# A newly searched order and engine choice for an attention and mixing kernel of 2292 operations

## The chip, the cores and the metric

The kernel runs on one core of a Trainium2 chip. It uses TensorE (PE) for matrix products, VectorE (DVE), ScalarE (ACT) and GpSimd (POOL) for elementwise work, and SyncE (SP) to issue all DMA transfers. The metric is device microseconds of one execution; the three runs of the kernel before gave 484.78, 487.29 and 488.31 us.

## The reference

Block attention over 4 batches, 8 heads, 768 positions and 64 columns a head: each query sees its neighbours within 15 positions and one summary (maximum of the keys, mean of the values) of each block of 32. The result `x` of 4 x 768 x 512 goes through a mixing layer:

```python
theta = x @ w_theta
zr, zi = x * cos(theta), x * sin(theta)
y = w_tok_r @ zr + w_tok_i @ zi          # over the 768 positions
u = x + y
return u + maximum(u @ w_ch, 0.0)
```

The weights `w_theta`, `w_tok_r`, `w_tok_i` and `w_ch` arrive as 64-bit floats and are turned into 32-bit ones by integer operations on the device.

## The kernel before

Every product that needs full precision is made of three matmuls on operands that are split in two: a high part, which is a cast of the 32-bit number to the matmul's reduced format, and a low part, the number minus its high part. So each operand costs a cast (`hi_op`, lines 307 on ScalarE and 309 on VectorE or GpSimd) and a subtraction (`lo_op`, line 316, on VectorE or GpSimd).

The work goes through these stages, overlapping each other:

- Loading and preparing. `to_f32` (lines 399 to 410) turns the weights into 32-bit numbers: an absolute value (399 on ScalarE, 401 on VectorE), a clamp (403), a shift (405), and two joinings (407 and 410).
- Attention, 24 tiles of 128 queries: scores (line 521), the running maximum (557), the exponential (561), transposes (570) and their copy out (574), the product with the values (544), normalising (582 to 591). Keys and values are copied into place by lines 493 and 498.
- Theta and the turn, per tile: transposes of `x` (600), their copies (307, 309, 606), the product with `w_theta` (631, 636), the reduction of the angle (647 to 655), sine and cosine (659, 660), the product with `x` (666).
- Mixing. The first two batches take the plain product (line 694). The last two use a scheme with seven products instead of eight (`mix_fast`, line 809): its operands are made in tiles `zu` by sums and differences (`add_op`, line 722) and split into tiles `hl`; its weights come back from a scratch tensor into the tiles `wt`; the results are added to `x` by line 818.
- Output. The product with `w_ch` uses seven products too (`out_batch`, line 914): operands are made from `u` by line 722 into tiles `cb` and split into tiles `wt`. For the first two batches `u` is loaded back into tiles `cu`; for the last two it is still in `x`. The channel weights are combined in the same way (tiles `zu`, `cb`, `wth`). The sums of the products are formed by lines 921 and 926, and line 933 makes the final result, which SP writes out.

An operand of the output is ready only when its cast and its subtraction are done; the products of line 914 and then the evictions of lines 921 to 933 wait for them. The banks in PSUM in which the products of line 809 gather are freed by line 818.

What sets the order is the table `ORDER`: each word is the number of an operation, in the order in which the program issues them; every engine takes its own in that order and does not pass a waiting one. A letter behind a number chooses the engine (`a` ScalarE, `d` VectorE, `g` GpSimd); without one the engine with the smallest assumed cost is taken:

```python
for word in ORDER.split():
    o = self.ops[int(word.rstrip("padg"))]
    o.eng = dict(p="PE", a="ACT", d="DVE", g="POOL").get(word[-1]) or min(o.cost)
    order.append(o)
```

When the instructions are laid down, a GpSimd operation that works on SBUF alone and follows directly, among such operations, on one of VectorE gets a wait for it (`port` in the last loop of `attn_moe`):

```python
if o.eng in o.port:
    mine = [i for i in traced[n:] if i.engine == units[o.eng]]
    if o.eng == "POOL" and port:
        tc.add_manual_dep(mine[0], port.name, ...)
    port = mine[-1] if o.eng == "DVE" else None
```

Of the kernel before, what the change touches and what calls it, by code (L numbers as in the profile page):

```python
# [54 lines left out]
23 0 1 24 14 8 27 17g 18 9 31 2 25 29 10 3 4 39 28 79 26 44g 5 33 30 32 19 6g 35 20 46g 45 49 7g 15 50 239 48g 47g 80d 190g 51  # L55
60 61 62 52 21 192g 11 81g 54 55 34 65 53 66 194g 63 82 86 36 64 67 185 193g 59 12 40 238g 83 191 87 42 56 37 93 84 38g 235 58
100 188 88 195 57 13 89 90 186 43 70 41 68 69 71d 204 206 295g 207 211 94 72 205 208 107 91 73d 293g 196 210 241g 76 240g 199
108 198 200 197 290 74 294g 22 77 95g 209 187g 202 92g 203 189g 242 75d 78d 237 96 201 214 212 223 243 101 215 97 246 245 213
236 102g 296g 98 216 85g 244 350g 103 99g 111 224 104 251 348g 225 247 118 254 119g 105 217 226 252 253 255 227 248 220d 218
106g 250 292 221 256 228 219d 249 123 222d 124g 349g 257 258 259 120 705g 229 261 121 262 297 125 260 230 270 126 298 231 263  # L60
300 271 272 304 122 273 109 306 308 345 110 309 301 307 141 291 264 265 267 268 113 351g 302 142g 274 299 266d 305 310 313 303
130 275 112 312 311 131g 707g 127 276 269d 314 143 316 144 315 419 317 352 135 277 325 318 132 326 136g 709g 232 286g 327 422g
133 347 328 329 114 425g 319 145 115 278 134 152 361 279 153g 362 128 353 330 355 146 116 147g 366 233 137 364 356 282 320 234
322 154 280 359 357 155 423g 283 346 138 284 323 285 363 339 367 139 281 368 156 331 354 321d 157 337 158g 324 338 424g 148
163 360 365 358 529 159 369 164g 149 332 371 380 150 160 370 372 426 165 381 333 420 421 334 373 427 166 400 382 161 167 374d
383 168 117 404 435 401 377 378 384 385 386 375 169g 170 174 340 335 171 175g 394 474 392 387 376 379 405 140 179 454 703g 393
# [12 lines left out]
700 818 676 702 728 649d 651 675 652d 840 795 819 580g 844g 686 684 685 687 796 753 850 725g 688 689d 1020 756 577 820 757 821
690 765 851g 766 975 691 761 581 729 730 800 822 1015 767 759 694 852g 845g 731 732 1021 976d 797 945 977 695 768 582 946 978  # L80
760 771 692 846d 979 770 801 693d 847g 823 802 980 758 769 726 848 853 749 762 764 763 804 772 981 824 803 854 806 849 573 810
855 750 798g 982 856g 696 943 941 775 983 776d 773 859 860g 861g 826d 947 774 984 956 777 960 805 995 825 948 862g 808 778d
828 996 858 829 799g 998 781 959 997 957 809 999 830 952 751 951 1000 857 1018 1001 949 958 950 831 782 953 779 963 961 863g
962 868 780d 985 955 954 811 783d 944d 1022 1023 986 964 966 1019 942g 1002 864g 967d 965 865g 1026 991 968 1003 827 866 1025
969 1004 1050 1031 1033 869g 870 993 1053 1051 1016 992 970 871g 1052 972d 867 877 807 1037 872g 1076 1024 1054 1027 1035 994
1074 1034 873 987 1129 1028 988 973 1077 1055 1030 878g 1038 1032 971 1036 989g 875 1005d 974d 1013 879 1056 1029 1041 1039
1057 1042d 1011 1058 1106g 1078 1017g 1059 874g 1079 1040 1170 1043 876 990g 886 1173 1120g 880g 1006 1208 1209 1211 1087 1047
1080 1060 1081 1044d 881 1088 1127 1210 1012 1082 1091 1014 1084 882g 1128 1083 1085 884 1089 1212 1048 1007 887 1092 1090
1045 1008 1086 1066 1046 888g 1075 1213 883 1049d 889g 1009g 1068 1214 1094 1126 1107g 1095 885 1093 895 1061 1097 1215 1096d
1067 1098d 1216 1010 890g 1062 891g 1130 1099 1217 1218 1219 896 893 1279 892g 1069 1131 1282 1139 1100 1064 1134 1070 1133  # L90
1143 1072 1280d 1140 1281 1135 897 1142 1132 1221 1144 1065g 1141 1145 1283 1101 1073 894 1284 1285 904 1136 1063 1103 898
1137 1102d 1247 899g 1138 1146 1071 1286 900g 1104 1158 1105d 901 1287 1149 1147 905g 906g 1174 1150 1148d 1288 1151 907 1305
1108 1152 1183 1220 1306 1110 1175 1121g 1185 1308 1171 1172 903 1153 1307 1179 1154d 908g 1309 1178 1176 1109 1177 909 902
910g 1184 1181 1250 1310 1155 1187 913 912 1111 1182 1289d 1156 1311 1180 1157d 1164g 1186 914g 1188 1189 1191 1118 1251 1190
1193 915g 1192 1116 1112 1312 1114 1313 911 916g 922 1122 1194d 1260 917g 1195 918g 1314 1199 1252 1262 1354 1123 1124 1125
1256 1355d 1159g 923 920 1357 919 921 1290 1162 924g 925g 1356 1358 1113 926 1315 1253 1257 931 1222 1165 1292 1249 927g 1160
1291 1196 1255 928g 929 1161 1359 1163 1197 1261 1265 1360 1223g 1168 1266 1228 1254 932g 1200 1202d 1316 933 1361 1166 1167
1264 1169 1263 1362 1258 1259 1198d 1599g 1267 1201d 1320 1268 1363 934g 1318 1593 1368 1270 1364 935g 1229 1204 1369d 930
1322 1370 1600g 1371d 1230 1248 936 1206 1372 1203g 938 1365 1271d 1231 1205 1317 1236 1373 937 1207 1237 1234 1117 1587g 1269
1374 1672 1594g 1366 1235 1232 1272 1240 1588g 1226 1227 1273 1276 1375 1376 1277 1274 1377 1275 1233 1295 1224 1278d 1319  # L100
1367 1225 1417 1418 1324g 1420 1325 1378d 1238 1293 1241 1294 1419 1421 1242 1385 1387 1296 1422 1379 1297 1589g 1301 1675
1595g 1302 1644 1243 1645 1299 1303 1423 1646 1424 1239 1244 1326 1425 1603g 1647 1658 1590 1388 1426 1327 1596g 1660 1427
# [1012 lines left out]
```

## Time and profile before

| | |
|---|---|
| runs | 484.78, 487.29, 488.31 us |
| the profiled execution | 484.78 us; its span, from the first to the last instruction, 483.0 us |
| TensorE (PE) busy | 440.1 us (91%) |
| VectorE (DVE) busy | 391.3 us (81%) |
| ScalarE (ACT) busy | 254.3 us (53%) |
| GpSimd (POOL) busy | 271.3 us (56%) |

Busy times are those of the engines' own instructions; waits and the issuing of DMAs do not count. A row of the windows gives them for one stretch. A row of the groups gives the line, the engine, the operation, what it writes and reads, the count, the busy time, the mean duration of one in ns, and the idle time of the engine ahead of them with what ended it. PEclk is the granted TensorE clock as a share of its full level.

### The profile page before, as it was taken

The page shows a single profiled execution, that of the slowest core. Times are in us where ns is not written, and L with a number is a line of the kernel's source. Part 1 is how long each engine was busy: PE and PEld are TensorE (multiplying, and loading weights), DVE is VectorE, ACT ScalarE, POOL GpSimd, SP SyncE. Part 2 cuts the span into 40 slices and gives each one's busy share as a digit, 9 for nine tenths or more (in the row PEclk, how much of TensorE's full clock was granted, in tenths as well). Part 3 has the DMA queues.
Part 4 walks back from the last instruction along what each step waited for, and adds up shares of the span by engine and source line. Part 5 has one row for each costly group of instructions (what it writes and reads, how often), then busy time and mean ns, then how long its engine had stood idle before and what let it go on. Part 6 is the DMA issues. An engine that isn't in the chain of part 4 may idle for free. (4 is left out here: it accounts for less than half of the span.)

```text
span 483.0 us, 9649 instructions
## 1 busy us (share of the span) xinstructions
PE 440.1 (91%) x3490; PEld 363.4 (75%) x3490; DVE 391.3 (81%) x940; ACT 254.3 (53%) x534; POOL 271.3 (56%) x262
## 2 busy tenths in 40 slices
PE   5969999999989999999999999999994966995997
PEld 1446555667868888888889899989894866985896
DVE  3899999798599565886768867667999989888896
ACT  1769886665578678756835534784420311331030
POOL 3595522636295646565532973231557788599550
PEclk9999999999999999999999999999997988998899
DMA  8999767897847798666688869441954744010037
GB/s 299 314 299 339 261 219 227 245 339 230 288 138 214 223 249 262 192 195 196 199 267 262 264 200 269 148 153 58 359 161 166 247 145 131 16 67 0 34 127 280
DMA packets 76318, 100.03 MB, mean 207 GB/s; under 512 B 23024, under 2 KB 58864, under 8 KB 76272
## 3 DMA queue, kind: packets, MB, share of 16 engines
q1 hardware_dynamic: 76272, 99.43, 65.4%
q8 instruction: 27, 0.44, 0.4%
q14 instruction: 19, 0.16, 0.1%
HBM read 75.82 MB, written 23.59 MB: 206 GB/s over the span
## 5 line engine op out<-in xcount | busy, mean ns | idle before, releaser
L809 PE MATMUL m<-wt,hl 128*128 128x384 f32 x504 | 99.3, 350 | 8.2 <-DVE x L818 8.0
L809 PEld LDWEIGHTS m<-wt,hl 128*128 128x128 f32 x504 | 91.5, 196 | 11.7 <-DVE x L818 8.1
L694 PE MATMUL m<-wt,hl 128*128 128x512 f32 (+1 forms) x432 | 83.7, 340 | 0.0
L694 PEld LDWEIGHTS m<-wt,hl 128*128 128x128 f32 x432 | 68.2, 188 | 10.7
L561 ACT ACTIVATE e<-e,st 128x118 f32<-128x118 f32 x192 | 62.8, 386 | 18.5 <-DVE st L557 18.0
L557 DVE CUSTOM_DVE_ANT_0 e<-s,cs 128x118 f32<-128x118 f32 x192 | 45.7, 272 | 11.4 <-PE s L521 10.3
L316 POOL TENSOR_TENSOR hl<-zu,hl 128x512 fp32r<-128x512 f32 x32 | 43.5, 1365 | 17.8 <-DVE hl L309 8.5
L636 PE MATMUL t<-wth,xh 128*128 128x512 f32 x144 | 47.1, 408 | 0.1
L722 POOL TENSOR_TENSOR zu<-zu 128x512 f32<-128x512 f32 x22 | 30.1, 1373 | 23.2 <-DVE zu L666 12.0
L666 DVE TENSOR_TENSOR zu<-xn,zu 128x512 f32<-128x512 f32 x48 | 37.2, 788 | 3.3 <-ACT zu L660 3.1
L722 POOL TENSOR_TENSOR f<-f 128x192 f32<-128x192 f32 x35 | 22.9, 656 | 29.8 <-DVE zu L666 13.9
L309 POOL CAST hl<-zu 128x512 fp32r<-128x512 f32 x24 | 16.0, 670 | 36.1 <-PE m L809 17.2
L694 PE MATMUL m<-wt,zu 128*128 128x512 f32 (+1 forms) x96 | 33.1, 491 | 0.5 <-DVE zu L666 0.4
L647 ACT ACTIVATE zu<-t,bmagic 128x512 f32<-128x512 f32 x24 | 16.5, 687 | 30.6 <-PE t L636 25.2
L307 ACT CAST hl<-zu 128x512 fp32r<-128x512 f32 x23 | 14.2, 617 | 32.0 <-PE m L809 17.7
L570 PE MATMUL pa<-cs,e 128*118 128x128 f32 x192 | 26.5, 275 | 4.6 <-DVE xn L591 2.8
L544 PEld LDWEIGHTS pa<-v,e 118*64 118x64 f32 x768 | 24.6, 137 | 6.9 <-issue 3.3
L544 PE MATMUL pa<-v,e 118*64 118x65 f32 x768 | 28.1, 224 | 1.5 <-ACT e L574 0.8
L694 PEld LDWEIGHTS m<-wt,zu 128*128 128x128 f32 x96 | 17.6, 190 | 15.7 <-issue 12.6
L316 DVE TENSOR_TENSOR hl<-zu,hl 128x512 fp32r<-128x512 f32 x28 | 27.7, 996 | 2.0 <-ACT hl L307 1.5
L570 PEld LDWEIGHTS pa<-cs,e 128*118 128x118 f32 x192 | 21.4, 136 | 10.1 <-issue 2.6
L636 PE MATMUL t<-wth,xl 128*128 128x512 f32 x72 | 28.5, 395 | 0.0
(189 smaller groups left out, 975.2 us busy)
## 6 DMA issues: line engine op xcount, KB each, us to landing
wt<-s_scratch SPq DMA_DIRECT2D x48, 384.0 KB, 4.8
v<-vg SPq DMA_DIRECT2D x48, 195.0 KB, 4.3
s_scratch<-f SPq DMA_DIRECT2D x24, 384.0 KB, 3.1
k<-kg SPq DMA_DIRECT2D x18, 376.0 KB, 5.3
q<-qg SPq DMA_DIRECT2D x24, 256.0 KB, 4.3
wt<-wtr SPq DMA_DIRECT2D x6, 768.0 KB, 10.7
wt<-wti SPq DMA_DIRECT2D x6, 768.0 KB, 11.8
f<-kT SPq DMA_DIRECT2D x12, 384.0 KB, 3.5
```

The costliest lines, as they stand in the source:

```text
L309: V[e].tensor_copy(dst(), src())
L316: lambda e: V[e].tensor_tensor(dst(), src(), hi().bitcast(F32), op=ALU.subtract), reads, writes, due, port=BOTH)
L544: mm(2 * 0.433 + scores[0] + (0.2 if scores[0] else 0.0), [lambda n=n, g=g, a=a: nc.tensor.matmul(xa[a].get()[ROW[g], n], turned[a].get()[ ...
L557: op({"DVE": 0.205}, lambda eng, n=n: nc.vector.tensor_tensor_reduce(e()[:, n], sc[n % 2].get()[:, 2 * a + n // 2], mask(m), -SCALE, 3.0e3 ...
L561: op({"ACT": 0.288}, lambda eng, n=n: nc.scalar.activation(e()[:, n], e()[:, n], AF.Exp, bias=st.get()[:, n:n + 1], scale=-1.0), [(st, n)] ...
L570: mm(NH * 0.109, [lambda n=n: nc.tensor.transpose(tp.get()[:NK, n], e()[:, n], ident()) for n in range(NH)], [e_ref, (cs, "ident")], [tp], ...
L636: calls = [lambda t=t, xx=xx, k=k, c=c: nc.tensor.matmul(th.get(), xx.get()[:, c], w_th[c].get()[:, k], start=(c == 0 and t == 0), stop=(c ...
L647: op({"ACT": 0.59}, lambda e: nc.scalar.activation(r(), th.get(), AF.Identity, bias=bmagic.get(), scale=1.0), [th, bmagic], R, due)
L666: op({"DVE": c_dve(DM, "two")}, lambda e, z=z, hc=hc: nc.vector.tensor_tensor(z(), xn[b, i].get().rearrange("p h d -> p (h d)")[:, None, h ...
L694: nc.tensor.matmul(acc[th](), zz, w[:, TT[th]], start=(s == 0 and r == 0 and t == 0 and (th == 0 or c == 0)), stop=(s == NT - 1 and r == 1 ...
L722: lambda e: V[e].tensor_tensor(dst(), x(), y(), op=ALU.add if sign > 0 else ALU.subtract), reads, writes, due, port=BOTH)
L809: calls = [lambda ref=ref, tt=tt, z=z, s=s, j=j, t=t, x=x, k=k, bank=bank, first=first: nc.tensor.matmul(bank[j].get()[:, :HT], z.get()[:, ...
```

## The change

Only the table `ORDER` is changed: all its 86 lines are new. The operations are the same 2292; their order differs, and 312 of them stand on another engine. In the built program GpSimd has 193 instructions where it had 267, ScalarE 621 where it had 536, VectorE 958 where it had 942; TensorE has 2641 and SP 289 in both.

```diff
 ORDER = """
-23 0 1 24 14 8 27 17g 18 9 31 2 25 29 10 3 4 39 28 79 26 44g 5 33 30 32 19 6g 35 20 46g 45 49 7g 15 50 239 48g 47g 80d 190g 51
...
-2263 2283 2168 2285 2203 2279 2267 2289 2268 2284 2286 2280 2287 2290 2288 2269 2291 2270
+17 31 23 25 0g 24 1g 27 29 18 11g 39 8g 19 26 44 20 28 46 45 9 2 33 86 10 48 3 30 4 5 49 21 190g 35 79 6g 47 185 32 7g 50 51
...
+2269 2270
 """
```

The engines' own orders show what that means. The first place is on GpSimd, where the operands of the last fast mix (`hl`, `zu`) end and the operands of the output stage (`cb`, `cu`, `wt`, `wth`) begin. Before:

```order
L722 TENSOR_TENSOR cb<-cu 128x768
L722 TENSOR_TENSOR zu<-zu 128x2x256
L316 TENSOR_TENSOR hl<-zu,hl 128x512
L309 CAST hl<-zu 128x512
L316 TENSOR_TENSOR hl<-zu,hl 128x512
L722 TENSOR_TENSOR zu<-zu 128x2x256
L309 CAST hl<-zu 128x512
L309 CAST wth_4516<-zu 128x512
L722 TENSOR_TENSOR cb<-zu 128x2x256 x2
L316 TENSOR_TENSOR hl<-zu,hl 128x512
L722 TENSOR_TENSOR cb<-cb,zu 128x2x256
L309 CAST wt<-cb 128x768
```

After, the same place, to near the end of GpSimd's queue:

```order
L722 TENSOR_TENSOR zu<-zu 128x2x256
L316 TENSOR_TENSOR hl<-zu,hl 128x512
L316 TENSOR_TENSOR wt<-cu,wt 128x768
L316 TENSOR_TENSOR wt<-cb,wt 128x768
L316 TENSOR_TENSOR wt<-x,wt 128x768
L722 TENSOR_TENSOR cb<-x,cb 128x768
L316 TENSOR_TENSOR wt<-cb,wt 128x768 x2
L316 TENSOR_TENSOR wt<-x,wt 128x768
L722 TENSOR_TENSOR cb<-x,cb 128x768
L316 TENSOR_TENSOR wt<-cb,wt 128x768
```

The casts and the channel weights have left GpSimd, and from the last `hl` on it keeps subtractions and a few differences.

The second place is on ScalarE, where its casts for the last fast mix (`hl`) give way to those for the output stage. Before:

```order
L307 CAST hl<-zu 128x512 x3
L307 CAST wth_4539<-zu 128x512
L307 CAST hl<-zu 128x512
L307 CAST wth_4584<-cb 128x512
L307 CAST wt<-cu 128x768
L307 CAST hl<-zu 128x512
L307 CAST zu<-zu 128x512
L307 CAST wt<-cb 128x768 x2
L307 CAST xh<-cb 128x512
L307 CAST hl<-zu 128x512
L307 CAST wt<-cu 128x768
L307 CAST wt<-x 128x768
```

After:

```order
L307 CAST hl<-zu 128x512 x5
L307 CAST wth_4546<-zu 128x512
L307 CAST hl<-zu 128x512
L307 CAST zu<-cb 128x512
L307 CAST wt<-cu 128x768
L307 CAST hl<-zu 128x512
L307 CAST wt<-cu 128x768
L307 CAST wt<-cb 128x768
L307 CAST hl<-zu 128x512 x2
L307 CAST wth_4645<-cb 128x512
L307 CAST wt<-cb 128x768
L307 CAST hl<-zu 128x512
```

ScalarE takes casts into `hl` and `wt` that stood on the two other engines.

The third place is on VectorE, where the channel weights are done (`wth`) and the first output operands are made. Before:

```order
L818 TENSOR_TENSOR x<-m_4263,x 128x384
L316 TENSOR_TENSOR wth_4516<-zu,wth_4516 128x512
L309 CAST zu<-cb 128x512
L316 TENSOR_TENSOR hl<-zu,hl 128x512
L316 TENSOR_TENSOR zu<-cb,zu 128x512
L309 CAST wt<-cu 128x768
L316 TENSOR_TENSOR wth_4584<-cb,wth_4584 128x512
L316 TENSOR_TENSOR hl<-zu,hl 128x512
L309 CAST hl<-zu 128x512
L316 TENSOR_TENSOR wt<-cu,wt 128x768
```

After:

```order
L722 TENSOR_TENSOR cb<-zu 128x2x256 x2
L316 TENSOR_TENSOR hl<-zu,hl 128x512
L316 TENSOR_TENSOR wth_4546<-zu,wth_4546 128x512
L722 TENSOR_TENSOR cb<-cu 128x768
L722 TENSOR_TENSOR cb<-cb,zu 128x2x256
L316 TENSOR_TENSOR zu<-cb,zu 128x512
L316 TENSOR_TENSOR hl<-zu,hl 128x512
L316 TENSOR_TENSOR wt<-cu,wt 128x768
L818 TENSOR_TENSOR x<-m_4315,x 128x384
L818 TENSOR_TENSOR x<-m_4377,x 128x384
L722 TENSOR_TENSOR cb<-cu,cb 128x768
```

VectorE takes the differences (line 722) that stood on GpSimd and gives its casts (line 309) to ScalarE.

## Rows read from the trace of the kernel before

**Rows 1.** The page: span, busy time by engine, chain that ended last.

```profile
span 483.0 us, 9649 instructions
...
PE 440.1 (91%) x3490; PEld 363.4 (75%) x3490; DVE 391.3 (81%) x940; ACT 254.3 (53%) x534; POOL 271.3 (56%) x262
...
PE 9%; DVE 6%; issue 2%; POOL 1%; ACT 0%; ACTq 0%; POOLq 0%
```

**Rows 2.** Windows: length; PE, PEld, DVE, ACT, POOL busy (count); PEclk; DMA share; GB/s.

```profile
0.00:106.40 106.40, 93.88 (x799) 53.77 (x800) 91.58 (x274) 71.45 (x157) 53.53 (x79) 1.00 0.88 281
106.40:342.40 236.00, 232.34 (x2105) 200.65 (x2104) 176.30 (x517) 151.53 (x325) 125.60 (x126) 1.00 0.71 214
342.40:480.40 138.00, 113.87 (x589) 108.95 (x587) 123.41 (x151) 31.30 (x53) 92.18 (x58) 0.93 0.40 139
```

**Rows 3.** The chain in order of time: start us, us, what.

```profile
417.64 1.04 PE c L914 x6
```

**Rows 4.** TensorE's waits from 342.4 us: for whom; us, times, longest us.

```profile
PE m L809 <- DVE x L818: 8.0, 3, 6.4
PE m L914 <- DVE x L818: 4.4, 1, 4.4
PE t L914 <- DVE wt L316: 3.9, 1, 3.9
```

**Rows 5.** Windows of two slices of 12 us, columns as in rows 2.

```profile
360.00:372.00 12.00, 5.61 (x25) 5.29 (x24) 12.00 (x13) 1.81 (x3) 9.35 (x7) 0.83 0.64 214
...
396.00:408.00 12.00, 7.58 (x38) 7.29 (x37) 12.00 (x10) 1.87 (x3) 10.14 (x6) 0.90 0.59 190
```

**Rows 6.** Timeline: start us, us, engine, line, operation, out<-in, count, idle before.

```profile
394.67 0.94 DVE L316 TENSOR_TENSOR wt<-cb,wt 128x768 fp32r<-128x768 f32 x1
...
399.38 2.10 POOL L316 TENSOR_TENSOR wt<-cu,wt 128x768 fp32r<-128x768 f32 x1 [0.90 <-DVE cb L722]
...
399.69 2.61 DVE L316 TENSOR_TENSOR wt<-cb,wt 128x768 fp32r<-128x768 f32 x1
```

**Rows 7.** Tail window of lines 316, 309, 722 (DVE, POOL), 933, 407 (DVE).

```profile
342.40:480.40 138.00, 38.03 (x32) 41.70 (x22) 0.93 0.40 139
...
342.40:480.40 138.00, 12.75 (x11) 14.16 (x14) 0.93 0.40 139
...
342.40:480.40 138.00, 16.02 (x11) 36.02 (x20) 0.93 0.40 139
...
342.40:480.40 138.00, 20.56 (x32) 0.93 0.40 139
...
342.40:480.40 138.00, 6.52 (x4) 0.93 0.40 139
```

**Rows 8.** VectorE groups from 342.4 us whose instructions ran alone.

```profile
L722 DVE TENSOR_TENSOR cb<-cu,cb 128x768 f32<-128x768 f32 x1 | 0.9, 946 | 0.0
...
L316 DVE TENSOR_TENSOR xl<-cb,xh 128x512 fp32r<-128x512 f32 x1 | 0.7, 680 | 0.0
...
L933 DVE SCALAR_TENSOR_TENSOR x<-t,x 128x384 f32<-128x384 f32 x1 | 0.6, 550 | 0.0
L309 DVE CAST wt<-x 128x768 fp32r<-128x768 f32 x1 | 0.5, 545 | 0.0
...
L309 DVE CAST zu<-cb 128x512 fp32r<-128x512 f32 x1 | 0.4, 413 | 0.0
```

**Rows 9.** GpSimd groups from 342.4 us.

```profile
L316 POOL TENSOR_TENSOR wt<-cb,wt 128x768 fp32r<-128x768 f32 x10 | 20.0, 2002 | 10.3 <-DVE wt L316 6.9 <-DVE x L933 2.2 <-DVE cu L933 0.6
L316 POOL TENSOR_TENSOR hl<-zu,hl 128x512 fp32r<-128x512 f32 x7 | 11.6, 1658 | 1.3 <-DVE hl L309 0.8 <-DVE zu L403 0.5
```

**Rows 10.** A ScalarE group from 342.4 us.

```profile
L307 ACT CAST wt<-cb 128x768 fp32r<-128x768 f32 x7 | 5.9, 839 | 15.8 <-DVE cb L722 8.8 <-POOL cb L722 5.3 <-PE m L809 1.3
```

**Rows 11.** Window of an early slice, columns as in rows 2.

```profile
36.00:48.00 12.00, 11.92 (x150) 7.67 (x143) 11.93 (x32) 11.86 (x26) 6.80 (x7) 1.00 1.03 340
```

**Rows 12.** A ScalarE group of the first 106.4 us.

```profile
L498 ACT COPY k<-zu 128x188 f32<-128x188 f32 x4 | 1.3, 344 | 2.5 <-PE s L521 2.5
```

More of the change, by code (lines that the diff above doesn't have):

```diff
@@ new lines @@
+1141 1110 1136 1247 1100d 1135 892g 1283 1101 1111 1142 1284 1102d 1172 1104 1071 1285 893 1108 1146 1140 896 1105 1144 897
+1128 1116 898g 899 1107g 1143 900d 1134 1109 1118 1286 1137 1145 894 1120 904 1149 1138 901g 1221 1147 903 1287 1250 1112
+1150d 1288 1174 1183 1148 1151 1114 1305 905 1185 1175 1122 1186 1123 902 906 1177 907 1121g 908 1308 1306 1152 1187 1289 1307
+1220 1164g 1190 1176 1249 1153 1155 1179 1248 913 1178 909g 1184 1189 910 911 1309 1154 1182 1156 1157d 1188 1124 1160 912
@@ new lines @@
+929 1599g 1204 1364 1226 930 1273 1371 1369 1274 1365 1316 931 1370 1366 1236 1385 1237 1372 1205 932g 1367 1324 1275 1240
+1242 1373 1318 1224 1374 1593 1277 1227 1375 1376 1278d 1317 1383 1600g 1594g 1225 1588g 1295 1377 933 1417 1589 1418 1293
+1420 1603 1325 1387 1419 1294 1590g 1421 1296 1422 1297 1378 1644 1243 1301 1299 1388 1595g 1303 1423 1379 1645 1380 1604g
+1424 1647 934g 1681 1326 1646 1648 1425 1381 1426 1335 1427 1238 1658 1327 1328 1322 1649 1428 1338 1239 1596g 1660 1429 1332
+1591d 1592 1330 1339 1337 1342 1651 1650 1329 1336 1672 1597d 1662 1431 1302 935 1653 1241 1664 1430 1611 1652 1341 1655 1678
@@ new lines @@
+1442 1464 1415 1529 1445 1613 1530 1433 1446 1412 1440 1447 1617d 1620 1413 1632 1448 1685 1614 1680 1687 1531 1683 1686 1619
+1432 1688 1441 1621 1439 1532 1451 1495 1416d 1689 16 1449 1692 1450 1443 1533 1704 1452 1453 1691 1454 1534 1698 1622g 1623g
+1455 1618 1535 1694 1695 1690 1536 1467 1476 1456 1465 1537d 1460 1573 1624g 1693 1697 1576 1700 1574 1468 1696 1538 1575
+1457d 1577 1479 1471 1701 1707 1726 1699 1478 1703 1578 1629 1480 1539 1475 1702 1625g 1540 1541 1635g 1706 1472 1477 1461
@@ new lines @@
+1524 1721 1542 1728 1521d 1548 1634g 1738 1554 1731 1556 1733 1736 1734 1737 1555 1549 1781d 1782 1783 1552 1547 1560 1784
+1640 1638g 1586 1637 1551 1553 1585 1522 1740 1779 1639 1785 1739 1752 1525 1559 1778 1746 1543 1786 1523d 1558 1743 1787
+1526d 1557 1550 1561 1641g 1758 1788 1749 1562 1564 1755 1742 1563 1789 1745 1565 1744 1723 1794 1566 1761 1747 1748 1642g
+1567d 1790 1795 1797 1796 1798 1791 1725 1907 1834g 1751 1568 1569 1570 1799 1643g 1750 1792 1824g 1571 1800 1825 1801 1802
+1753 1793 1572 1838 1822g 1803 1754 1756 1804 1759 1808 1809 1835 1757 1823g 1762 1760 1763 1811 1810 1812 1805 1839g 1764
```

150 lines of the change are left out of this document (66 added, 84 removed).

## The prediction

> **What bounds the kernel now.** I read the page first, then the windows, then TensorE's waits, then single instructions. TensorE is busy 440.1 of 483.0 us [rows 1], so only its idle time and its slowed stretches can be won back, and the question is where they lie. Three windows say it [rows 2]. Up to 106.4 us (loading, preparing the token weights, the first batch's attention) TensorE works 93.88 us. From 106.4 to 342.4 us it works 232.34 of 236.0 us: nothing is to be had there. From 342.4 us, the end of the last theta product, to 480.4 us it works 113.87 of 138.0 us. I call this last window the tail. It holds the fast mix of the fourth batch and all of the output stage: 252 matmuls of line 809 and 336 of line 914. Six such matmuls in an unbroken run take 1.04 us [rows 3], so 588 of them are 102 us of work; the tail is 36 us longer than that. Part of the difference is the 24.1 us that TensorE stands still, part is matmuls at a low clock after such pauses (a mean granted clock of 0.93 in the tail against 1.00 before it [rows 2] and 0.83 in the slice from 360 us [rows 5]: a mixture of the two levels, 2.4 and 1.2 GHz).
>
> Whom does it wait for? The three longest entries of TensorE's waits in the tail are all VectorE, 16.3 us together [rows 4]. And VectorE is full: 123.41 us of the 138.0, and 12.00 of 12.00 in both slices shown, while TensorE has 5.61 and 7.58 there [rows 2, 5]. GpSimd is busy 92.18 us in the tail, ScalarE only 31.30 [rows 2].
>
> VectorE is full because its instructions are stretched. The same line-316 subtraction of 768 columns takes 0.94 us at 394.67 and 2.61 us at 399.69, where a GpSimd subtraction has been running since 399.38 and ends at 401.48 [rows 6]: the second one got through 0.82 us after GpSimd let go. To size this for the tail I set what each line cost against its lone price [rows 7, 8]. Line 316: 32 instructions, 15 of 768 columns at 0.94 and 17 of 512 at 0.68, would be 25.7 us alone and took 38.03. Line 309: 7 at 0.545 and 4 at 0.413 make 5.5, took 12.75. Line 722: 5 at 0.946 and 6 at 0.68 make 8.8, took 16.02. Line 933: 32 at 0.55 make 17.6, took 20.56. Line 407: 4 at 0.68 make 2.7, took 6.52. The excess is 12.3 + 7.3 + 7.2 + 3.0 + 3.8 = 33.6 us, which is 0.36 us of VectorE for each of GpSimd's 92.2 us.
>
> **The change, part by part.** It adds and removes no work: TensorE has the same matmuls in nearly the same order, each operation the same form or its twin on another engine. Three things move in the tail.
>
> GpSimd loses work. Counting the rows of the two orders in the tail: line 309 loses 12 casts (nine of 768 columns for the output operands), line 316 nine subtractions (two of 768, seven of 512), line 722 thirteen differences. At the means of GpSimd's own rows [rows 7, 9] that is 12 x 1.01 + 2 x 2.00 + 7 x 1.66 + 13 x 1.80 = 12.1 + 4.0 + 11.6 + 23.4 = 51 us of 92; 41 us stay.
>
> ScalarE gains casts: 14 of 768 columns for the output operands at 0.84 us [rows 10], six of 512 columns, an absolute value and two evictions more, about 17 us in all. With 31.30 us busy of 138.0 it has room; these cost nothing unless a cast stands in its queue behind an eviction that waits for a product. In the order the casts now stand between evictions (line 926), so such waits must be expected; the cover is ScalarE's 90 us of slack.
>
> VectorE gains nine subtractions (two of 768, seven of 512 columns) and thirteen differences (seven of 768, six of 512), and gives up about eight casts, two evictions and one absolute value. At lone prices [rows 8] that is 1.9 + 4.8 + 6.6 + 4.1 = 17.4 us more and 5.8 less: +11.6 us. What such an instruction costs in the new company no row shows. It is bounded by 0.946 us alone and 2.6 us beside GpSimd for 768 columns; I take the lone price here and carry the company as stretch. If the stretch keeps its rate, 41 x 0.36 = 15 us remain of 33.6: -18.6. The balance on VectorE is -18.6 + 11.6 = **-7.0 us**.
>
> Beside that, the chain of waits gives GpSimd 1% of the span, 4.8 us [rows 1], for subtractions and differences of which more than half move to an engine that takes half as long (0.946 against 2.0 us): 2 us. So the tail becomes about 138 - 9 = 129 us. TensorE's own 102 us stay below that, so VectorE is still late next, only less.
>
> Ahead of the tail I put nothing. Up to 106.4 us VectorE is busy 91.58 us [rows 2], and there the two orders give it nearly the same instructions; GpSimd is relieved of some copies, ScalarE takes them. Between 106.4 and 342.4 us a relief of VectorE is hidden under TensorE's 232 of 236 us; a new wait there would show at once, since there is no slack. SP's queue keeps its shape in the tail: the four channel weights, then reloads of `cu` between loads of `wt` that wait for products. Before, three reloads stood ahead of six such loads and the fourth behind them; now two stand ahead of seven and two behind. The third reload is needed only by the second difference of the first output batch, which stands well down VectorE's queue, so I put nothing; if it came late, that difference and all behind it on VectorE would wait.
>
> A rule to weigh. The pair above is a turn-taking: the later instruction had its own length left when the earlier one ended [rows 6]. The Trainium skill, SBUF — State Buffer, section "Who interferes with whom", states it as an exclusive lock: a Vector instruction with two SBUF inputs and a GpSimd instruction that reads SBUF do not share, the second waits the first one out. The trace agrees, 2.61 us for a 0.94 us instruction. By that rule the stretch need not keep its rate: it vanishes wherever no GpSimd instruction is open, and the rival of the larger gain below would be the forecast. By the row totals 0.36 us per us is what it was on average, with GpSimd open for two thirds of the tail; I keep the average.
>
> Sum: the profiled execution took 484.8 us, 1.8 more than its span. 484.8 - 9 = **476 us**. The median of the three runs, 487.3, is 2.5 above that execution; I leave the forecast on the execution whose rows I summed and let the range carry the 2.5.
>
> **The rivals.**
> A, slower: the stretch does not go. GpSimd's remaining 41 us stand between VectorE's two-input instructions, which are now more (22 moved there), so each open GpSimd instruction may find one to hold. Place: VectorE from the first output operand to the last. If none of the 33.6 us went, the tail would be 11.6 us longer: 496 us. It turns to a loss when less than 11.6 of the 33.6, a third, goes. Against it: GpSimd's time falls by more than half.
> B, no change: the gain is given back early. ScalarE is busy 11.86 of 12 us from 36 to 48 us [rows 11] and now gets some seven more key copies (0.344 us [rows 12]) and several value copies and evictions in the first third, 5 to 7 us. If it becomes what the first attention tiles wait for, 9 - 6 leaves 3 us: 482 on the same execution, 484 to 485 against the runs' median. Against it: over the first 106.4 us ScalarE is busy 71.45 and VectorE 91.58 [rows 2].
> C, a larger gain: in the order, GpSimd has no instruction between the fourth batch's last operand and the first output operand's subtraction, just where the full slices lie. If VectorE runs alone there and the whole stretch goes, the balance is 11.6 - 33.6 = -22 us, the tail 116 us, still above TensorE's 102: 463 us.
>
> **How the numbers follow.** The forecast's case (471 to 481 us) has 0.50, C 0.17, B 0.18, A 0.15. A difference of 1%, 4.9 us, is about what a measurement of this kernel can tell. Against the median of 487.3, faster means under 482.4: nearly all of the first case and all of C, 0.65; within 1%: B and a rest of the first, 0.19; slower: A and an early loss that outweighs the tail, 0.16. For 8 in 10 the range reaches to C and to half of A: 464 to 490 us. The likeliest case alone has 471 to 481.
>
> **What would show it.** In the changed profile: GpSimd's busy time in the tail near 41 us and ScalarE's near 48; line 722 on VectorE with some 24 instructions in the tail; line 316 of 768 columns nearer 1.2 than 1.5 us on average; fewer waits of line 809 for line 818. If VectorE's tail is under 105 us, C holds. If its line-316 mean stays near 1.5 us, A. If the window to 106.4 us has grown by 5 us, B. The forecast is wrong if the middle window shows new TensorE waits, or if the tail stays at 138 us with VectorE idle: then something else than VectorE set it.

## The result

The changed kernel takes 445.5 us, median of 4 runs (444.26 to 445.90); the kernel before took 486.03 beside it. The ratio is 0.9158, 95% interval 0.9111 to 0.9204: 41 us less, where 9 were forecast. The profiled execution took 445.88 us, its span is 444.1 us; it is 38.9 us shorter than the profiled execution before (484.78 us), and these are the 38.9 us that the windows below account for. Place and direction were forecast right, the size was not.

The page, as in [rows 1]:

```profile
span 444.1 us, 9625 instructions
...
PE 430.2 (97%) x3490; PEld 359.0 (81%) x3490; DVE 356.2 (80%) x956; ACT 288.3 (65%) x619; POOL 189.1 (43%) x188
...
PE 77%; DVE 12%; DMA 4%; POOL 2%; issue 2%; ACT 2%; SPq 1%; POOLq 0%; ACTq 0%
```

Of the chain that ended last TensorE has 77%. The shares of [rows 1] sum to 18% only: before, the chain could be followed back over the last 18% of the span and no further, so the two lines can't be compared by their numbers. Windows with nearly the same bounds in the program as [rows 2] (the middle one ends with the last theta product):

```profile
0.00:104.00 104.00, 95.25 (x801) 56.94 (x802) 88.62 (x268) 80.74 (x175) 46.99 (x68) 0.98 0.91 288
104.00:334.50 230.50, 230.50 (x2104) 200.50 (x2103) 168.15 (x529) 161.06 (x370) 102.81 (x98) 1.00 0.72 218
334.50:441.50 107.00, 104.41 (x588) 101.57 (x587) 99.41 (x161) 46.53 (x75) 39.29 (x22) 1.00 0.52 182
```

The tail fell from 138.0 to 107.0 us, against the 102 us that its 588 matmuls need in an unbroken run [rows 3]; the two windows ahead of it gave 2.4 and 5.5 us. In the tail TensorE stands still 2.6 us instead of 24.1, and the same matmuls take 104.41 us instead of 113.87, at a mean granted clock of 1.00 instead of 0.93: 21.5 + 9.5 = 31.0 us. VectorE is busy 24.0 us less and idle 7.6 us instead of 14.6. The waits of TensorE that answer to [rows 4] are gone; the longest of the tail are now

```profile
PE m L809 <- ACT hl L307: 0.7, 1, 0.7
PE m L809 <- issue: 0.6, 1, 0.6
PE m L809 <- DVE hl L316: 0.4, 1, 0.4
```

Two slices in which VectorE is full, as in [rows 5]. It is as full as before, and TensorE doesn't wait:

```profile
372.00:384.00 12.00, 12.00 (x71) 12.00 (x70) 12.00 (x18) 7.30 (x12) 2.00 (x1) 1.00 0.69 231
388.00:400.00 12.00, 12.00 (x70) 11.71 (x69) 11.93 (x20) 6.90 (x11) 6.87 (x3) 1.00 0.05 19
```

And the tail by line (316, 309, 722 on VectorE and GpSimd, then 933 and 407 on VectorE), as in [rows 7]:

```profile
334.50:441.50 107.00, 33.99 (x41) 24.02 (x12) 1.00 0.52 182
...
334.50:441.50 107.00, 1.92 (x4) 0.61 (x1) 1.00 0.52 182
...
334.50:441.50 107.00, 19.30 (x23) 12.29 (x7) 1.00 0.52 182
...
334.50:441.50 107.00, 19.05 (x32) 1.00 0.52 182
...
334.50:441.50 107.00, 2.65 (x4) 1.00 0.52 182
```

Line 316 now has 41 instructions on VectorE, nine more than before, and takes 33.99 us instead of 38.03. At the lone prices of [rows 8] its 17 of 768 and 24 of 512 columns make 16.1 + 16.3 = 32.4 us. The stretch is nearly gone, though GpSimd is still busy 39.29 us. Why it is gone is what the experiments ask.

### The profile page after: what moved, and what is told of

Same layout as the page of the kernel before. It is cut to its first block, busy times and chain, and to the rows that moved or that the text cites. A ratio compares the mean times of both kernels' runs of the same rounds, so it can differ in the third digit from the quotient of the medians.

```text
span 444.1 us, 9625 instructions
## 1 busy us (share of the span) xinstructions
PE 430.2 (97%) x3490; PEld 359.0 (81%) x3490; DVE 356.2 (80%) x956; ACT 288.3 (65%) x619; POOL 189.1 (43%) x188
## 4 chain that ended last, share of the span: by engine, by line
PE 77%; DVE 12%; DMA 4%; POOL 2%; issue 2%; ACT 2%; SPq 1%; POOLq 0%; ACTq 0%
PE m L694 19%; PE m L809 18%; PE t L636 11%; PE c L914 7%; PE m L914 6%; PE pa L544 4%; PE s L521 4%; PE pa L570 4%; PE t L600 3%; DMA q<-qg 2%; DVE f L407 2%; DMA wth<-wth 2%; DVE wt L410 2%; DVE zu L666 2%; DVE f L405 1%
## 5 line engine op out<-in xcount | busy, mean ns | idle before, releaser
L809 PE MATMUL m<-wt,hl 128*128 128x384 f32 x504 | 95.7, 340 | 1.8 <-ACT hl L307 0.7
L809 PEld LDWEIGHTS m<-wt,hl 128*128 128x128 f32 x504 | 87.5, 188 | 5.7 <-issue 1.4
L694 PEld LDWEIGHTS m<-wt,hl 128*128 128x128 f32 x432 | 68.2, 188 | 10.8 <-DVE v L493 0.2
L316 POOL TENSOR_TENSOR hl<-zu,hl 128x512 fp32r<-128x512 f32 x26 | 35.2, 1361 | 50.9 <-PE pa L544 12.0
L666 DVE TENSOR_TENSOR zu<-xn,zu 128x512 f32<-128x512 f32 x48 | 35.7, 760 | 12.3 <-ACT zu L660 12.1
L307 ACT CAST hl<-zu 128x512 fp32r<-128x512 f32 x30 | 18.6, 620 | 21.0 <-PE m L809 13.0
L521 PE MATMUL s<-k,q 64*64 64x118 f32 x768 | 25.7, 268 | 6.1 <-DMA q<-qg 3.3
L574 ACT COPY e<-pa 118x512 f32<-118x512 f32 x35 | 19.8, 585 | 16.6 <-PE pa L570 16.5
L694 PEld LDWEIGHTS m<-wt,zu 128*128 128x128 f32 x96 | 17.8, 190 | 14.9 <-issue 12.9
L521 PEld LDWEIGHTS s<-k,q 64*64 64x64 f32 x768 | 19.9, 132 | 12.0 <-issue 3.5
L570 PEld LDWEIGHTS pa<-cs,e 128*118 128x118 f32 x192 | 22.6, 140 | 5.6 <-issue 2.3
L309 POOL CAST hl<-zu 128x512 fp32r<-128x512 f32 x20 | 13.6, 678 | 31.6 <-DVE zu L666 8.6
## 6 DMA issues: line engine op xcount, KB each, us to landing
wt<-wti SPq DMA_DIRECT2D x6, 768.0 KB, 11.6
```

Source lines behind the costliest of these rows:

```text
L316: lambda e: V[e].tensor_tensor(dst(), src(), hi().bitcast(F32), op=ALU.subtract), reads, writes, due, port=BOTH)
L521: mm(0.79 * len(pairs) / NP, [lambda p=p, g=g, h=h: nc.tensor.matmul(sc[h].get()[ROW[g], p], q.get()[ROW[h], p, ROW[g]], k.get()[ROW[h], p ...
L570: mm(NH * 0.109, [lambda n=n: nc.tensor.transpose(tp.get()[:NK, n], e()[:, n], ident()) for n in range(NH)], [e_ref, (cs, "ident")], [tp], ...
L574: lambda e: (nc.scalar.copy if e == "ACT" else nc.vector.tensor_copy)(t.get()[:NK], tp.get()[:NK].rearrange("k n q -> k (n q)")), [tp], [t ...
L666: op({"DVE": c_dve(DM, "two")}, lambda e, z=z, hc=hc: nc.vector.tensor_tensor(z(), xn[b, i].get().rearrange("p h d -> p (h d)")[:, None, h ...
L694: nc.tensor.matmul(acc[th](), zz, w[:, TT[th]], start=(s == 0 and r == 0 and t == 0 and (th == 0 or c == 0)), stop=(s == NT - 1 and r == 1 ...
```

## Experiments

**Two theories.** The forecast rested on the amount: each microsecond of GpSimd stretches VectorE by 0.36 us, wherever it lies. The rival is the place: only certain VectorE instructions are stretched, and the order decides which of them GpSimd meets. The trace of before already had a case against the amount (timeline: start, us, engine, line):

```profile
404.70 0.54 DVE L818 TENSOR_TENSOR x<-m,x 128x384 f32<-128x384 f32 x1
405.17 0.54 DVE L926 COPY zu<-c 128x384 f32<-128x384 f32 x1
405.63 1.66 DVE L316 TENSOR_TENSOR hl<-zu,hl 128x512 fp32r<-128x512 f32 x1
...
404.92 1.82 POOL L316 TENSOR_TENSOR wt<-cb,wt 128x768 fp32r<-128x768 f32 x1 [0.96 <-DVE wt L316]
```

Beside the same GpSimd instruction (404.92 to 406.74) lines 818 and 926, which read a product from PSUM (`m`, `c`), keep their 0.54 us, and the line-316 subtraction, with both inputs in SBUF, takes 1.66 us for its 0.68.

So for each kernel I went through the instructions of the tail, from the end of the last theta product to the end of the last matmul. For every VectorE instruction the overlap is the part of its duration in which a GpSimd instruction was running, the excess is its duration less that of the same form alone ([rows 8], and for the forms not shown there the duration of those without company). "Product" are instructions with an input in PSUM, "SBUF" all others. All in us:

| kernel | time | tail | GpSimd | overlap SBUF | overlap product | excess SBUF | excess product |
|---|---|---|---|---|---|---|---|
| before | 486 | 137.3 | 92.1 | 62.3 | 22.8 | 37.5 | 0.1 |
| changed | 445.5 | 106.2 | 39.5 | 13.6 | 23.6 | 5.5 | 0.0 |
| head_after | 474.4 | 136.4 | 91.3 | 62.3 | 22.0 | 36.9 | 0.1 |
| tail_after | 458.0 | 109.9 | 40.8 | 14.4 | 24.0 | 6.3 | 0.1 |
| tail_old_engines | 480.6 | 141.2 | 93.5 | 64.0 | 18.8 | 37.9 | 0.0 |
| tail_new_engines | 473.8 | 123.6 | 48.3 | 33.6 | 12.0 | 16.2 | 0.1 |
| pool_beside_sbuf | 457.0 | 118.6 | 39.3 | 25.3 | 12.0 | 17.4 | 0.1 |
| no_turns | 470.9 | 119.6 | 40.1 | 26.6 | 12.3 | 15.6 | 0.1 |
| casts_back | 451.8 | 113.4 | 56.4 | 29.2 | 24.3 | 11.1 | 0.0 |
| diffs_back | 467.8 | 128.9 | 90.4 | 47.0 | 24.4 | 29.0 | 0.1 |
| before_no_turns | 493.4 | 142.4 | 91.4 | 67.8 | 17.5 | 42.1 | 0.1 |

(An overlap holds the stretched part too. The sums are good to about 1 us: they depend on the lone durations chosen and on the instructions at the edges. The excess of before is 37.5 here and 33.6 in the prediction, which counted five lines only.)

**Early part or tail.** Two splices of the two tables, cut at TensorE's last theta product:

```diff
 head_after:
-ORDER = old table
+ORDER = changed table up to the cut, with its engines; behind it the old table's rows
 tail_after:
-ORDER = old table
+ORDER = old table up to the cut; behind it the changed table's rows, with its engines
```

> The changed order and engines for every operation up to the fourth batch's last theta product; behind it the old order and the old engines. Theory of sums (the two stretches add up): the early stretch brings its 8 us (486 - 8 = 478 us) and the tail keeps its 138 us, with VectorE's excess over lone prices near 33 us. Rival (the early gain is only a start that the tail hands back, because the tail waits for reloads or for GpSimd): 483 us or more, the tail grown to 143 us.

> The old order and the old engines up to the fourth batch's last theta product, the changed ones behind it. Theory of sums: the tail shrinks from 138 to 107 us by itself, 486 - 31 = 455 us. Rival (the tail needs the earlier hand-over of the changed early part, such as operands made before the tail begins): the tail stays above 115 us, 463 us or more.

Measured: 474.44 us (ratio 0.9746, 0.9696 to 0.9795) and 457.97 us (0.9407, 0.9350 to 0.9463). The early part brings 11.9 us, the tail 28.4, together 40.3 of the 41: the two add up, and neither rival holds. With the changed early part the old tail keeps its 136.4 us and its excess of 36.9.

**Order or choice in the tail.** The changed order with the tail's operations back on their old engines, and the old order with the tail's operations on their new ones. A letter behind a number puts that operation on an engine (`d` VectorE, `g` GpSimd, `a` ScalarE); 73 operations of the tail differ, such as

```diff
 tail_old_engines, against the changed kernel:
-... 2178 ... 2233 ... 2177 ... 2188d ...
+... 2178g ... 2233g ... 2177g ... 2188g ...
 tail_new_engines, against the kernel before: the same words the other way round
```

> The changed order everywhere, but in the tail every operation is back on the engine that it had before: the order alone. GpSimd is back near 92 us in the tail. Amount theory (0.36 us of VectorE's time per us of GpSimd's): VectorE's excess is back at 33 us, the tail at 138 us, 478 us. Place theory (VectorE is stretched only where a GpSimd instruction lies beside an instruction that has no product as an input, some 0.65 us per us of such overlap): in the new order GpSimd's slots lie beside 27 us of instructions that read products, as they did before, so 92 - 27 us must again lie beside the others or in VectorE's gaps; excess 25 to 40 us, 470 to 480 us. The two agree here; the run is for how much the order does by itself. Rival: the order alone does most of it, 455 us or less.

> The old order everywhere, but in the tail every operation on the engine that the change gives it: the choice of engines alone. GpSimd is near 40 us in the tail. Amount theory: 40 x 0.36 = 15 us of excess on VectorE stay, the tail near 129 us, 477 us. Place theory: the excess is 0.65 us per us in which GpSimd lies beside VectorE's instructions that read no product; in the changed kernel this overlap is 9 us, and where the old order leaves GpSimd beside the same kind of instruction as before (50 of 92 us) it would be 22 us, 14 us of excess. Beyond that the old order, made for other engines, can leave instructions late on ScalarE and VectorE: 470 to 480 us. Rival: the choice of engines alone does all of it, 458 us or less.

Measured: 480.63 us (0.9870, 0.9816 to 0.9925) and 473.81 us (0.9736, 0.9672 to 0.9801). Against head_after the new order alone loses 6 us; TensorE there waits 9.1 us at one place for a subtraction on GpSimd (in this kernel and in tail_new_engines the lines are numbered two higher: 916 is 914, 318 is 316):

```profile
PE m L916 <- POOL wt L318: 9.5, 2, 9.1
```

The choice alone wins 12.5 us in the old order, near the 9 that I had forecast for the whole change: GpSimd's time is halved, and the excess is more than halved (16.2 of 37.5). Both theories had that (15 and 14 us), so this run doesn't decide between them.

```profile
343.80:468.20 124.40, 108.23 (x589) 102.99 (x587) 112.98 (x164) 46.24 (x75) 49.35 (x23) 0.99 0.44 155
```

VectorE is still the fullest engine in that window, 112.98 of 124.40 us, and 12.9 of TensorE's 16.2 idle us there are waits for it. The other 16 us (473.8 to 458.0 us) come only when order and choice stand together.

**The place, at a constant amount.** Fourteen of the changed kernel's 22 GpSimd instructions of the tail get other neighbours on VectorE; every engine keeps its instructions, GpSimd keeps its queue. One of the moves (2173 is a subtraction of line 316 on GpSimd, 2078 a line-933 instruction with both inputs in SBUF, 2174 a difference of line 722 on VectorE):

```diff
-2000 2123 2087 1999 2078 2128 2174 2088 2173g 2131
+2000 2123 2087 1999 2173g 2078 2128 2174 2088 2131
```

> The changed kernel with fourteen of the tail's 22 GpSimd instructions put elsewhere between the same neighbours on GpSimd's queue: each now begins where VectorE's next instructions have only SBUF inputs. Every engine has the same instructions, GpSimd's 39 us stay. Amount theory: nothing depends on the place, excess near 5 us, 445 us. Place theory: by the trace of the changed kernel the overlap of lone durations goes from 6 to 20 us, each such pair makes VectorE wait the GpSimd instruction out, so the excess rises from 5 us to 15 to 22, VectorE comes to 115 us or more in the tail and passes TensorE's 104: 452 to 458 us.

Measured: 456.99 us (0.9377, 0.9354 to 0.9400), 11.5 us more than the changed kernel. GpSimd's 39 us haven't changed, the excess went from 5.5 to 17.4, as the place theory had it (15 to 22 us; 452 to 458 us); only VectorE's busy time, 111 us, stayed under the 115 named with it. By the amount theory nothing should have happened. Neither TensorE nor VectorE waits for GpSimd anywhere in this tail, so it isn't that the moved instructions deliver late; most of TensorE's waits are for VectorE again. The window of the tail, the three longest of these waits, and the pair that the move above made:

```profile
333.30:452.70 119.40, 109.28 (x589) 104.58 (x587) 111.12 (x161) 46.33 (x75) 39.00 (x23) 0.97 0.47 164
```

```profile
PE m L914 <- DVE zu L921: 2.7, 2, 2.4
PE c L914 <- DVE cu L933: 2.1, 1, 2.1
PE m L809 <- ACT hl L307: 1.5, 2, 0.8
```

```profile
392.12 1.01 DVE L818 TENSOR_TENSOR x<-m,x 128x384 f32<-128x384 f32 x2
393.05 2.17 DVE L933 SCALAR_TENSOR_TENSOR cu<-zu,cu 128x384 f32<-128x384 f32 x1
...
392.94 1.86 POOL L316 TENSOR_TENSOR wt<-x,wt 128x768 fp32r<-128x768 f32 x1
```

The line-933 instruction takes 2.17 us. In the changed kernel the same GpSimd instruction has other company:

```profile
392.81 2.45 POOL L316 TENSOR_TENSOR wt<-x,wt 128x768 fp32r<-128x768 f32 x1 [1.43 <-DVE cb L722]
...
392.59 0.94 DVE L316 TENSOR_TENSOR wt<-cb,wt 128x768 fp32r<-128x768 f32 x1
393.46 0.55 DVE L933 SCALAR_TENSOR_TENSOR cu<-c,cu 128x384 f32<-128x384 f32 x1
393.93 0.54 DVE L921 TENSOR_TENSOR zu<-c,zu 128x384 f32<-128x384 f32 x1
394.40 0.57 DVE L921 TENSOR_TENSOR m<-m,zu 128x384 f32<-128x384 f32 x1
394.87 1.21 DVE L316 TENSOR_TENSOR wt<-cu,wt 128x768 fp32r<-128x768 f32 x1
```

Three instructions that read products go by at full pace while GpSimd runs; only the subtraction of 394.87 waits, 0.26 us.

**The turn.** Both kernels have a line that lets a GpSimd instruction wait for the VectorE instruction emitted ahead of it. It guards no data:

```diff
-                if o.eng == "POOL" and port:
+                if False:
```

> The changed kernel without the line that makes a GpSimd instruction wait for the VectorE instruction emitted ahead of it; that wait guards no data. Same order on every engine, same engines. Amount theory: 445 us, or a little less, since GpSimd starts earlier. Place theory: GpSimd's instructions begin as soon as their inputs are there, so more of their 39 us fall beside VectorE's instructions with only SBUF inputs; if half of them do, overlap 20 us and excess 12 us, 447 to 452 us.

> The kernel before without the line that makes a GpSimd instruction wait for the VectorE instruction emitted ahead of it. In the changed kernel that line was worth 25 us. If the waits are what puts GpSimd's instructions beside the right VectorE instructions, it is worth less in the kernel before, where 62 of GpSimd's 92 us lie beside the wrong ones anyway: 485 to 495 us. Rival (the line keeps GpSimd from running ahead in any order): 505 us or more.

Measured: 470.85 us (0.9665, 0.9627 to 0.9702) for the changed kernel without it, 493.38 us (1.0162, 1.0100 to 1.0225) for the kernel before. The line is worth 25.4 us after the change and 7.7 before it. The direction is the place theory's, the size in the changed kernel I had far too small. In the tail the excess rose by 10 us, about as expected, and the tail by 13.4. The rest, 10.7 us, was lost ahead of the tail, which the expectation had left out: the last theta product ends at 345.2 us instead of 334.5; the largest single piece is one wait of TensorE at a matmul of line 521, 5.3 us where the changed kernel has 1.2, for which the trace shows no releaser. Without the line in either kernel the change is still worth 22.5 us (493.38 to 470.85) instead of 40.5. So a good part of what the order gives rests on the wait that keeps GpSimd in its place, but not all of it.

**Which of the moved work.** In the changed order, the 13 casts that went to ScalarE back on GpSimd, or the 30 instructions that went to VectorE:

```diff
 casts_back:
-... 2183 ... 2248 ... 2186 ... 2236 ...
+... 2183g ... 2248g ... 2186g ... 2236g ...
 diffs_back:
-... 2178 ... 2233 ... 2188d ... 2185 ... 2234 ...
+... 2178g ... 2233g ... 2188g ... 2185g ... 2234g ...
```

> The changed kernel with the tail's 13 casts that went from GpSimd to ScalarE back on GpSimd (13 us there in the trace of before), each at the same place in the order. Amount theory: 13 x 0.36 = 5 us more on VectorE, which has 7 us to spare: 445 to 448 us. Place theory: the casts' places were not made for GpSimd; if half of their time lies beside VectorE's instructions with SBUF inputs, 4 to 6 us of excess more, and each cast is followed by a subtraction that waits for it: 447 to 453 us. Both are under 20% of the 35 us that the choice of engines is worth in the new order.

> The changed kernel with the tail's 30 instructions that went from GpSimd to VectorE (15 differences, 13 subtractions, two others; 53 us on GpSimd in the trace of before) back on GpSimd, each at the same place in the order. GpSimd near 92 us less the 13 of the casts, so 80 us or more, VectorE's lone sum near 85 us. If these are what the tail was bound by, most of the 35 us come back: 468 to 478 us, VectorE's excess 25 to 35 us. Rival (VectorE has the room either way, so only what stays in place counts): under 460 us.

Measured: 451.81 us (0.9297, 0.9256 to 0.9338) and 467.84 us (0.9619, 0.9570 to 0.9668). The casts cost 6.3 us of time and 5.6 of excess, as the place theory had it (447 to 453 us, 4 to 6 us) and more than the amount theory allowed; the differences and subtractions cost 22.3 us, just under the 468 to 478 us expected, with an excess of 29.0 us (25 to 35). With the latter VectorE isn't full:

```profile
334.70:464.40 129.70, 114.28 (x588) 108.62 (x587) 102.53 (x131) 46.11 (x75) 89.02 (x52) 0.92 0.43 150
```

VectorE is busy 102.53 us, 3.1 more than in the changed kernel, and the tail is 22.7 us longer. Here it isn't the sum on VectorE that decides. TensorE's waits in that trace:

```profile
PE m L914 <- ACT wt L307: 5.0, 2, 3.9
PE m L914 <- POOL wt L316: 3.1, 1, 3.1
...
PE c L914 <- POOL wt L316: 1.8, 1, 1.8
```

They are for operands that end on GpSimd, or on ScalarE in line 307, which rounds what a difference has made. Which part of the 22 us is GpSimd's longer duration and which is the stretch, this run can't tell.

**The early part.** The same questions ahead of the tail, each with the old tail: the changed table up to the second batch's first theta product only (the recorded expectation calls it the first batch's last; that one, of line 631, ends at 98.98 us in the kernel before, and the cut and the 112.1 us are those of the next, the first of line 636), the choice of engines alone, the order alone.

```diff
 first_after:       changed table up to the second batch's first theta product, then the old table
 early_new_engines: old order; ahead of the tail the changed table's letters
 early_new_order:   changed order ahead of the tail; every operation on its old engine
```

> The changed order and engines up to the first batch's last theta product (the first 112 us), the old ones behind it. The whole early part brought 11.9 us with the old tail. By the end times of the two traces the first 112 us hold 2.7 us of the early 7.9 and the rest comes later: 483 us. Rival (what is prepared early, weights and operands, is what the middle gains by): 479 us or less. Other rival (it was the middle that brought all, and the start is handed back): 486 us.

> The old order everywhere, the changed choice of engines up to the fourth batch's last theta product, the old choice in the tail. If the choice alone did the early part, 474 us as with the changed early order; if choice and order must come together, as in the tail, where the choice without the order brought 12.5 of 28 us, about half: 480 us. If the choice without its order puts instructions late on ScalarE in the full first 106 us, slower than 486 us.

> The changed order up to the fourth batch's last theta product, but every operation on its old engine; the old tail. Order and choice together gave 474.4 us with the old tail, the choice in the old order 510.5. If the early part goes like the tail (the order alone cost 6 us there), 490 to 510 us: TensorE's waits in the middle for VectorE and ScalarE grow above the 3.7 us of before. Rival (the early gain is the order's): 474 to 478 us.

Measured: 485.37 us (0.9973, 0.9953 to 0.9992), 510.45 us (1.0473, 1.0439 to 1.0507) and 510.95 us (1.0512, 1.0451 to 1.0573). Choice alone and order alone each lose some 24 us (23.5 and 25.3); together they win 11.9. The first part alone brings 1.6 us, near the second rival's 486, although its theta product at the cut ends 3.7 us earlier (108.4 instead of 112.1): the old middle hands it back, and in the two traces the last theta product ends even 1.1 us later (343.5 instead of 342.4). From the product at the cut to the end of the last one (kernel before; changed; choice alone; order alone; first part alone), columns as in [rows 2]:

```profile
112.10:342.40 230.30, 226.64 (x2085) 196.95 (x2084) 171.36 (x505) 147.14 (x312) 121.22 (x123) 1.00 0.70 212
```

```profile
109.40:334.50 225.10, 225.10 (x2086) 197.15 (x2085) 163.28 (x511) 156.68 (x353) 98.72 (x95) 1.00 0.73 221
```

```profile
114.00:365.40 251.40, 234.47 (x2086) 200.53 (x2085) 171.42 (x510) 160.09 (x357) 100.63 (x98) 0.98 0.64 194
```

```profile
119.60:371.90 252.30, 234.35 (x2086) 202.32 (x2084) 164.26 (x505) 142.68 (x308) 119.67 (x119) 0.97 0.66 200
```

```profile
108.40:343.50 235.10, 228.14 (x2086) 198.22 (x2084) 174.10 (x509) 147.26 (x312) 122.68 (x125) 0.99 0.70 209
```

TensorE's idle time is 3.7 us before, 0.0 in the changed kernel, 16.9 and 18.0 in the two halves and 7.0 with the first part alone. VectorE, ScalarE and GpSimd are busy at most 74% of any of these windows, so no engine's sum over the window explains the loss. In the two halves TensorE's waits there are spread over many places, the longest 3.3 and 3.5 us, about half of their time in each for ScalarE. That single instructions stand late in their queues is the likely cause; no run shows it.

## Why the prediction was right or wrong

Of the 30 us that the forecast missed, 17 are VectorE's busy time in the tail (24.0 less instead of 7.0), 7.0 its idle time there and 7.9 what came ahead of the tail, less the 2 that stood for GpSimd's chain.

**The bound: right.** TensorE's idle time in the tail was most of what could be won, and it was waiting for VectorE. When the stretch went, those waits went; when pool_beside_sbuf put 11.9 us of the stretch back, TensorE's idle time rose from 2.6 to 10.1 us (119.40 less 109.28), most of it for VectorE.

**The moved work: right.** GpSimd lost 52.9 us in the tail (51 forecast), ScalarE gained 15.2 (17). VectorE's instructions of the tail cost 93.3 us at lone prices before and 103.8 after: +10.5 (+11.6 forecast). VectorE has 23 instructions of line 722 (some 24). No wait for a cast behind an eviction is above 0.7 us, and no reload of `cu` is waited for in the tail.

**The stretch: wrong, and this is the step that failed.** "If the stretch keeps its rate, 41 x 0.36 = 15 us remain of 33.6" put one rate on all of GpSimd's time. What remained is 5.5 us of 37.5. In pool_beside_sbuf the same 39 us cost 17.4. So there is no rate per microsecond of GpSimd: it was 0.14 and 0.44 in these two. What counts is the time beside instructions whose inputs are all in SBUF: 0.60 us of excess per us of that overlap in the kernel before (37.5 / 62.3), 0.69 in pool_beside_sbuf, 0.40 in the changed kernel, 0.38 to 0.62 in the other experiments. That is a range and no price, since the overlap holds the excess itself, and since it is sometimes GpSimd that waits (last section). Beside instructions that read a product the excess was 0.1 us or less in every row of the table. The change took the first overlap from 62.3 to 13.6 us and left the second at 23. My 15 us are what the choice alone leaves in the old order (16.2). The average was the wrong step, and the trace of before could have said so: 22.8 us of GpSimd's time lay beside lines 818, 921, 926 and the product-reading 933 there, with no stretch at all.

**The rule that I weighed.** Beside GpSimd, line 933 keeps its 0.55 us with a product as its source and takes up to 2.21 with both inputs in SBUF. The Trainium skill, SBUF — State Buffer, section "Who interferes with whom", says that a Vector instruction with at most one SBUF input, outside the modes that use both ports, doesn't contend with GpSimd. The traces agree. By that rule the question would have been which instructions stand beside GpSimd in the new order. I had weighed the lock and then gone back to the average. That the second of a pair waits only the first one out, as I put it, is not what every pair shows: a GpSimd instruction can be held by several of VectorE's in a row (last section).

**VectorE's idle time: wrong.** I let the tail fall by as much as VectorE's work does. It fell by 24.0 us of VectorE's busy time (7.0 forecast) and by 7.0 of its idle time. About half of the latter is VectorE waiting less for TensorE (7.5 us before, 4.1 after), the rest waiting less for GpSimd and ScalarE (6.2 before, 2.1 after). TensorE's clock went with it: 9.5 of the 31 us are the same matmuls taking less, at 1.00 instead of 0.93.

**GpSimd's share of the chain: too small.** I took 2 us from its 1% of the span, in a chain that covers 18% of it. In diffs_back the moved differences and subtractions are worth 22 us, with VectorE only 3.1 us busier than in the changed kernel. A share of the chain that ended last doesn't tell what a slow engine's instructions cost when they make the operands that the next product needs.

**Ahead of the tail: wrong.** "Nothing is to be had there" stood beside 232.34 of 236.0 us: 3.7 us were idle, and all of them were won. With what the first part gave, 7.9 us were gained by the end of the last theta product, and head_after as a whole ran 11.9 us faster. Of the 5.2 us by which the middle got shorter, 3.7 are TensorE's idle time; for the other 1.5, matmuls whose time sums to less, I have no cause.

**The rivals.** C, the larger gain, came true by its own terms: a balance of -22 us on VectorE, -24.0 measured, and the sign that I gave for it, VectorE's tail under 105 us (99.41). Line 316 of 768 columns came to 1.03 us on average, below the 1.2 that I had named. C's tail of 116 us missed only the idle time. Its reason was half right: between the last operand of the fourth batch and the first of the output stage GpSimd is nearly empty (2.00 of 12 us from 372 us), but 23.6 of its 39 us lie elsewhere, beside product-reading instructions. A and B didn't happen in the change; both happen when one half of it is taken alone. The order without the choice leaves the stretch and slows the tail (A), and the choice without the order costs 23.5 us, lost ahead of the tail (B, but larger, and most of it behind the start: the middle is 21.1 us longer, 13.3 of them idle time of TensorE).

## What to carry to other kernels

Price GpSimd's work by what runs beside it on VectorE: go through the instructions by their inputs, and count only the overlap with those that read SBUF alone. Beside instructions that read products GpSimd's work cost VectorE nothing here, so a searched order should put it there, with a wait that keeps it there: in the changed order that wait was worth 25 us, 13 of them in the tail. And where order and engines change together, neither half's effect tells the whole: in the early part each half lost some 24 us and both won 12.

## What the runs showed of the hardware

Over the traces of before, changed, pool_beside_sbuf, no_turns and diffs_back, whole programs, by form: line 933 with a product as source, 54 instructions beside GpSimd, none above 0.56 us; with both inputs in SBUF, 32 beside GpSimd, mean 1.31, longest 2.21, median alone 0.56. Line 557, which reads scores from PSUM, 621 beside GpSimd, mean 0.270 us, median alone 0.274. Line 444, a reduction with one SBUF input, 45 beside GpSimd, mean 0.946, median alone 0.953. A cast is different, though it has one input too: line 309 of 768 columns, 11 beside GpSimd, mean 1.07, longest 2.21, median alone 0.556. So one SBUF input doesn't free an instruction; it depends on the operation.

The wait goes both ways. In pool_beside_sbuf:

```profile
389.45 0.95 DVE L722 TENSOR_TENSOR cb<-cu,cb 128x768 f32<-128x768 f32 x1
390.32 0.95 DVE L316 TENSOR_TENSOR wt<-cb,wt 128x768 fp32r<-128x768 f32 x1
...
389.61 3.38 POOL L316 TENSOR_TENSOR wt<-cb,wt 128x768 fp32r<-128x768 f32 x1 [7.32 <-DVE wt L309]
```

The GpSimd instruction takes 3.38 us, 1.5 more than the 1.86 of the next one, and both VectorE instructions keep their length, the second too, which began 0.7 us after GpSimd's. VectorE instructions in close order can thus hold GpSimd for more than one turn. The longest such case is in tail_new_engines (between the second and the third line stand five more VectorE instructions with both inputs in SBUF, each at its lone length):

```profile
388.56 0.95 DVE L318 TENSOR_TENSOR wt<-cb,wt 128x768 fp32r<-128x768 f32 x1
389.43 0.69 DVE L318 TENSOR_TENSOR wth<-zu,wth 128x512 fp32r<-128x512 f32 x1
...
394.11 0.95 DVE L318 TENSOR_TENSOR wt<-cb,wt 128x768 fp32r<-128x768 f32 x1
...
388.79 7.74 POOL L318 TENSOR_TENSOR hl<-zu,hl 128x512 fp32r<-128x512 f32 x1 [13.53 <-DVE wth L318]
```

The GpSimd subtraction of 512 columns, whose shortest is 1.25 us, takes 7.74 and ends 1.47 us after the last of these VectorE subtractions. Most of that time counts as overlap, and the wait in it is GpSimd's, not VectorE's: one reason why excess and overlap have no fixed ratio.
